# Windowed attention and a maxout FFN on one core: loading q and k chunk by chunk, and splitting attention units by query tile

## The chip, the cores and the metric

The kernel runs on one core of one Trainium2 chip. TensorE (PE) does the matmuls, VectorE (DVE) and ScalarE (ACT) the elementwise work and the copies out of PSUM, GpSimd (POOL) builds the masks and issues most loads, SyncE (SP) issues small copies and the stores. The metric is the device time of one execution in microseconds, lower is better. A profiled execution lists every instruction; its span runs from the first to the last of them.

## The reference

Attention over 4 batches, 8 heads, 768 positions of 64 elements, each query seeing the first 4 positions (sinks) and the last 128; then a feed-forward part with the maximum of three products:

```
scores = (1/8) * q @ k^T
keep   = (key < 4) | (0 <= query - key < 128)
a      = softmax(where(keep, scores, -1e9))
x      = (a @ v) laid out as 3072 tokens x 512
h      = max(x @ w1, x @ w2, x @ w3)          # 512 -> 768
out    = h @ w_out                            # 768 -> 512
```

Inputs and output are float32; the kernel computes in bfloat16 with float32 sums.

## The kernel before, in words

Tokens are cut into 12 chunks of 256 (three a batch). For each chunk there are two attention *units*, one for each group `g` of four heads. A unit's `scores` (L390) writes keys x queries for the four heads into one PSUM tile `st` of four banks, of which there is only one: four heads use four row groups of 32, with even and odd elements of a head dimension as two accumulating passes `e`. Columns 0 to 127 are the previous 128 keys for the first 128 queries, 128 to 383 the first key tile of the chunk for all 256 queries, 384 to 511 the second key tile for the second 128 queries. `exps` (L395, ACT) runs twice, for two heads each, over all columns; `masks` (L403, DVE) likewise multiplies by `mask`, or `mask0` in a batch's first chunk. `pv(tt)` (L412, L421, PE) makes values and row sums for 128 queries; it waits for both masks. `norm` (L431, L434, DVE) divides, `xt` (L444, PE) transposes, `xt_copy` (L451, ACT) stores into `xT`.

Sinks: from a batch's second chunk on, the four sink keys get their own scores (`sink_scores`, L344, exp L350), from `kbd` (L307, DVE), and their values from `vbd`, filled by sixteen small SP copies a batch (`sink_v`, L324).

The FFN works on *blocks* of chunks: `BLOCKS = [[0], [1, 2], [3, 4], [5, 6], [7, 8], [9, 10], [11]]`, so one of 256 tokens, five of 512, one of 256. `hgroup` (L510) makes 18 products a block; the first of each three is copied by ACT (`evac`, L519), the other two are taken into the maximum by DVE (L521). `ygroup` (L529) makes the output of 128 tokens, ACT copies it (L536) and SP stores it. A block's FFN needs the attention of all its chunks; the next block's attention runs beside it. Four PSUM buffers (`h_ring`) serve h, y, values, transposes and sink scores.

q and k must be transposed to put the head dimension on the partitions. DVE does it with 32 x 32 transposes of bfloat16 pairs taken as float32 (L286). Batch 0 is loaded in chunks of 256 tokens (`raw0`); its first chunk comes as float32, by SP for q and ACT for k, four copies for each head group (`qk_first`, L160), with a cast by DVE (L293) for q and ACT (L295) for k. Batches 1 to 3 come as whole loads of 768 tokens for each head group (`batch_loads`, L258), and then three transposes out of the tile, with destination steps of 24 elements where batch 0 has 8. Those loads and v (L172 by key tile in batch 0, L265 by four heads later) are issued by POOL, which casts to bfloat16 on the way.

The order on each engine comes from a planner. Every step is a `Task` with an engine, a cost, what it depends on and a due time `want`; `arrange` takes, over all engines, the task that can start earliest, and among those of one engine that can start about equally early the one with the smallest `want`. Loads are tasks of a model engine `DMA` with 0.30 MB/us (`rate`). Instructions are emitted in the order found, and each engine runs its own in order; at run time semaphores hold them to their true dependencies.

Of the kernel before, what the change touches and what calls it, by code (L numbers as in the profile page):

```python
# [87 lines left out]
def kernel(  # L88
# [35 lines left out]
    mask = const.tile([128, 512], BF16, name="mask")  # L124
# [6 lines left out]
    raw0 = {}  # L131
    for g in range(NQ):
        for nm in "qk":
            raw0["f", nm, g] = const.tile([128, 512], F32, name=f"{nm}_f{g}")
            raw0[nm, g] = const.tile([128, NC, 512], BF16, name=f"{nm}_first{g}")
# [10 lines left out]

    dma_done = {}
    rate = 0.30

    def load(name, mb, want, f, eng="POOL", cost=0.65, deps=()):  # L150
        t = task(eng, cost, f, deps=deps, want=want, name="i" + name)
        dma_done[name] = task("DMA", mb / rate, lambda: None, deps=[t], want=want, lat=2.0, name=name)
# [10 lines left out]
    def qk_chunk(nm, src, g, c):  # L163
        def f():
            s = src[0, 4 * g:4 * g + 4, 256 * c:256 * c + 256].rearrange("i (p j) d -> i p (j d)", j=8)
            nc.gpsimd.dma_start(out=raw0[nm, g][:, c, :], in_=s)
        return f
# [14 lines left out]
    for g in range(NQ):  # L182
        load(f"q0{g}0", 0.26, g - 2000, qk_first("q", q, g), eng="SP", cost=0.4)
        load(f"k0{g}0", 0.26, g - 2000, qk_first("k", k, g), eng="ACT", cost=0.4)
# [8 lines left out]
    for n in range(2):  # L193
        load(f"v0{n}", 0.26, nxt(), v_chunk(n), cost=0.9)
    ws = (moe_w1, moe_w2, moe_w3)
    for wi in range(3):
        load(f"w{wi}0", 0.52, nxt(), w_part(wi, ws[wi], 0, 2))

    def make_masks():
        nc.gpsimd.memset(mask, 1.0)  # L200
        m4 = mask.rearrange("p (t r q) -> p t r q", t=2, r=2)
        nc.gpsimd.affine_select(out=m4[:, :, 1, :], in_=m4[:, :, 1, :], compare_op=ALU.is_ge,
                                fill=0.0, base=0, pattern=[[0, 2], [1, 128]], channel_multiplier=-1)
        nc.gpsimd.affine_select(out=m4[:, :, 0, :], in_=m4[:, :, 0, :], compare_op=ALU.is_gt,
                                fill=0.0, base=0, pattern=[[0, 2], [-1, 128]], channel_multiplier=1)
        nc.gpsimd.tensor_copy(mask0, mask[:, 128:512])
        nc.gpsimd.memset(mask0[0:n_sink, 0:256], 1.0)
# [15 lines left out]
    t_bd = task("POOL", 0.6, make_bd, want=nxt(), name="bd")  # L223

    def chunk_loads(c):
        for g in range(NQ):
            load(f"q0{g}{c}", 0.26, nxt(), qk_chunk("q", q, g, c))
            load(f"k0{g}{c}", 0.26, nxt(), qk_chunk("k", k, g, c))
        for n in (2 * c, 2 * c + 1):
            load(f"v0{n}", 0.26, nxt(), v_chunk(n), cost=0.9)  # L230

    chunk_loads(1)
    for f0 in (2, 4):
        for wi in range(3):
            load(f"w{wi}{f0}", 0.52, nxt(), w_part(wi, ws[wi], f0, 2))
    chunk_loads(2)
    load("wo", 1.57, nxt(), lambda: nc.gpsimd.dma_start(
        out=wo_sb, in_=moe_w_out.rearrange("(a p) f -> p a f", p=128)))

# [5 lines left out]

    t_zero = task("DVE", 3.0, set_zeros, want=-1000, name="zero")


    raws, tr_done, sink_done, qTs = {}, {}, {}, {}
    last_pv = {}  # L250

    def batch_loads(b, after_tr, after_pv):

        for g in range(NQ):
            for nm, src in (("q", q), ("k", k)):
                def f(nm=nm, src=src, g=g):
                    raws[b, nm, g] = io.tile([128, 24, 64], BF16, name=f"{nm}_raw{g}", tag=f"{nm}_raw{g}")
                    nc.gpsimd.dma_start(  # L258
                        out=raws[b, nm, g].rearrange("p j d -> p (j d)"),
                        in_=src[b, 4 * g:4 * g + 4].rearrange("i (p j) d -> (i p) (j d)", j=24))  # L260
                load(f"{nm}{b}{g}", 0.79, nxt(), f, deps=after_tr)
        for hf in range(2):
            def fv(hf=hf):
                vv = vbufs[b % 2][:, 4 * hf:4 * hf + 4, :, :D].rearrange("p h n d -> p (h n) d")
                nc.gpsimd.dma_start(out=vv, in_=v[b, 4 * hf:4 * hf + 4].rearrange(  # L265
                    "h (n p) d -> p (h n) d", p=128))
            load(f"v{b}{hf}", 0.79, nxt(), fv, cost=1.4, deps=after_pv)

    def tile_T(b, nm, g):
        if (b, nm, g) not in qTs:  # L270
            qTs[b, nm, g] = io.tile([128, S, 2], BF16, name=f"{nm}T{g}", tag=f"{nm}T{g}")
        return qTs[b, nm, g]

    def transposes(b, g, part, want):

        for nm in ("q", "k"):
            def f(nm=nm):
                dst = tile_T(b, nm, g).rearrange("p s e -> p (s e)").bitcast(F32)
                if b == 0:
                    src = raw0[nm, g][:, part, :].bitcast(F32).rearrange("p (j c) -> p j c", j=8)  # L280
                    dst = dst[:, 256 * part:256 * part + 256].rearrange("p (m j) -> p j m", j=8)
                else:
                    src = raws[b, nm, g].rearrange("p j d -> p (j d)").bitcast(F32).rearrange(
                        "p (j c) -> p j c", j=24)[:, 8 * part:8 * part + 8, :]
                    dst = dst.rearrange("p (m j) -> p j m", j=24)[:, 8 * part:8 * part + 8, :]
                nc.vector.transpose(dst, src)  # L286
            deps = []
            if b == 0:
                deps.append(dma_done[f"{nm}0{g}{part}"])
                if part == 0:  # L290
                    def cast(nm=nm):
                        if nm == "q":
                            nc.vector.tensor_copy(raw0[nm, g][:, 0, :], raw0["f", nm, g])  # L293
                        else:
                            nc.scalar.copy(raw0[nm, g][:, 0, :], raw0["f", nm, g])  # L295
                    deps = [task("DVE" if nm == "q" else "ACT", 0.5, cast, deps=deps, want=want,
                                 name=f"cast{nm}{g}")]
            else:
                deps.append(dma_done[f"{nm}{b}{g}"])
                if b > 1:  # L300
                    deps += [s_done[b - 2, g, x] for x in range(NC)] + [es_done[b - 2, 1]]
            tr_done[b, nm, g, part] = task("DVE", 0.62, f, deps=deps, want=want,
                                           name=f"tr{nm}{b}{g}{part}")
        if part == 0:
            def sink_k():
                kv = tile_T(b, "k", g)[:, 0:n_sink, :].rearrange("p s e -> p e s")
# [5 lines left out]
            if b > 0:  # L312
                return sink_k
            sink_done[b, "k", g] = task("DVE", 0.2, sink_k, deps=[tr_done[b, "k", g, 0], t_bd, t_zero],
                                        want=want + 3, name=f"kbd{b}{g}")

    def sink_v(b, want):
# [10 lines left out]
        t = task("SP", 1.6, f, deps=deps, want=want, name=f"vbd{b}")  # L328
# [5 lines left out]
    def sink_scores(b, cs, want):  # L334
# [19 lines left out]
        for g in range(NQ):  # L354
            for c in (cs if b == 0 else range(NC)):
                deps.append(tr_done[b, "q", g, c])
        t1 = task("PE", 0.55, mm, deps=deps, want=want, lat=0.2, alloc=[h_ring], name=f"SK{b}{cs}")
# [8 lines left out]
    hs_ring = Ring(2, "hs")  # L366
    h_all, y_all, s_done, chain = {}, {}, {}, {}

    def unit(b, c, g, blk, off, w0, dw):

        lo = 128 if c == 0 else 0
        ncol = 512 - lo
        st = {}

        def scores():
# [3 lines left out]
            qT, kT = tile_T(b, "q", g), tile_T(b, "k", g)  # L379
            q0 = 256 * c  # L380
            parts = []
            if c > 0:
                parts.append((0, 128, q0 - 128, q0))
            parts.append((128, 256, q0, q0))
            parts.append((384, 128, q0 + 128, q0 + 128))
            for col, n, key0, qq in parts:
                for e in range(2):
                    for i in range(4):
                        r = slice(32 * i, 32 * i + 32)
                        nc.tensor.matmul(ps[:, i, col:col + n], lhsT=kT[r, key0:key0 + 128, e],  # L390
# [271 lines left out]
```

## Time and profile before

| | us |
|---|---|
| median of 3 runs (lowest, highest) | 203.46 (203.42, 204.44) |
| the profiled execution | 202.47 |
| its span | 200.7 |
| busy: PE, DVE, ACT, POOL | 172.7, 135.7, 95.1, 36.7 |
| PE busy of the first 16 us | 2.82 |
| mean granted TensorE clock | 0.983 |

A busy PE is not a PE at its peak: a matmul that runs at half clock, or waits inside the pipeline, counts as busy too. So work is priced by stretches in which nothing disturbs it, and holes by what came after them.

### The profile page before, as it was taken

How to read it: one execution, taken by the hardware profiler on the slowest of the kernel's cores; microseconds unless marked ns; L12 is line 12 of the kernel's file. 1: busy time of each engine (PE TensorE's matmuls, PEld its weight loads, DVE VectorE, ACT ScalarE, POOL GpSimd, SP SyncE). 2: the span in 40 equal slices, each digit the busy share in tenths (PEclk: the TensorE clock that was granted, in tenths of full speed). 3: DMA queues.
4: the chain of work that ended last, by engine and by line, in shares of the span. 5: the costliest groups of instructions: out<-in, count | busy, mean ns of one | idle time of the engine just before them, and what ended most of it. 6: DMA issues, size and time to landing. Idle time of an engine off the chain costs nothing.

```text
span 200.7 us, 4228 instructions
## 1 busy us (share of the span) xinstructions
PE 172.7 (86%) x1680; PEld 95.7 (48%) x1680; DVE 135.7 (68%) x290; ACT 95.1 (47%) x146; POOL 36.7 (18%) x56
## 2 busy tenths in 40 slices
PE   0127997588979997999998999989999989999892
PEld 0023676433445544455554455554555544454770
DVE  4358497587999999999917758636677276571450
ACT  0344562634447548434668245665266592223422
POOL 7997648233200000022000000000000000000000
PEclk9999999759999999999999999999999999999999
DMA  7999999999999910409920200140000410002202
GB/s 125 207 160 154 197 172 198 213 180 172 255 173 177 195 63 1 156 4 80 82 106 1 105 4 0 42 170 0 3 0 5 157 52 3 0 0 106 108 0 104
DMA packets 41012, 19.72 MB, mean 98 GB/s; under 512 B 29472, under 2 KB 35872, under 8 KB 40992
## 3 DMA queue, kind: packets, MB, share of 16 engines
q0 software_dynamic: 36256, 12.07, 56.8%
q1 hardware_dynamic: 4352, 6.85, 9.6%
q10 hardware_dynamic: 384, 0.52, 1.0%
q8 instruction: 13, 0.21, 0.4%
q14 instruction: 7, 0.06, 0.1%
HBM read 25.17 MB, written 6.29 MB: 157 GB/s over the span
## 4 chain that ended last, share of the span: by engine, by line
PE 66%; DVE 21%; DMA 5%; issue 3%; ACT 3%; SPq 1%; DVEq 0%; ACTq 0%
PE h L510 39%; PE y L529 13%; PE st L390 6%; DMA q_f<-in_q_dram 5%; DVE kT L286 4%; DVE h_sb L521 4%; DVE x L434 4%; PE o L421 4%; DVE e_sb L403 4%; DVE qT L286 3%; PE xt L444 2%; ACT e_sb L395 2%; PE o L412 2%; DVE rc L431 1%; SPq L160 1%
## 5 line engine op out<-in xcount | busy, mean ns | idle before, releaser
L510 PE MATMUL h<-xT,w_sb 128*128 128x512 bf16 (+1 forms) x504 | 103.7, 353 | 1.8 <-ACT xT L451 1.2
L521 DVE TENSOR_TENSOR h_sb<-h,h_sb 128x512 bf16<-128x512 f32 (+1 forms) x84 | 51.4, 616 | 26.1 <-PE h L510 20.3
L510 PEld LDWEIGHTS <-w_sb 128*128 128x128 bf16 x504 | 46.8, 99 | 38.5 <-issue 2.6
L395 ACT ACTIVATE e_sb<-st 128x1024 bf16<-128x1024 f32 (+1 forms) x48 | 44.4, 953 | 14.4 <-PE st L390 14.4
L519 ACT CAST h_sb<-h 128x512 bf16<-128x512 f32 (+1 forms) x42 | 22.1, 526 | 47.6 <-PE h L510 47.3
L529 PE MATMUL y<-wo_sb,h_sb 128*128 128x512 bf16 x144 | 33.9, 387 | 0.1
L403 DVE TENSOR_TENSOR e_sb<-e_sb,mask 128x1024 bf16<-128x1024 bf16 (+1 forms) x48 | 29.7, 640 | 5.1 <-ACT e_sb L395 4.9
L390 PE MATMUL st<-qT,kT 32*128 32x128 bf16 (+1 forms) x512 | 15.9, 253 | 16.5 <-DVE kT L286 9.3
L536 ACT COPY y_sb<-y 128x512 f32<-128x512 f32 x24 | 14.1, 586 | 21.5 <-PE y L529 17.6
L390 PEld LDWEIGHTS <-kT 32*128 32x128 bf16 x512 | 10.9, 98 | 25.0 <-DVE kT L286 9.9
L434 DVE TENSOR_TENSOR x<-o,rc 128x256 bf16<-128x256 f32 x48 | 20.4, 424 | 1.7
L431 DVE RECIPROCAL rc<-o 128x4 f32<-128x4 f32 x48 | 8.5, 177 | 19.2 <-PE o L421 19.2
L529 PEld LDWEIGHTS <-h_sb 128*128 128x128 bf16 x144 | 13.8, 99 | 15.5 <-issue 1.6
L421 PEld LDWEIGHTS <-e_sb 128*128 128x128 bf16 x352 | 17.4, 102 | 6.5 <-DVE e_sb L403 1.5
L421 PE MATMUL o<-v_sb,e_sb 128*128 128x65 bf16 x352 | 19.4, 201 | 1.1 <-DVE h_sb L521 0.6
L451 ACT COPY xT<-xt 128x512 bf16<-128x512 bf16 x24 | 14.1, 588 | 9.2 <-PE xt L444 9.1
L444 PE MATMUL xt<-ident,x 128*128 128x128 bf16 x96 | 12.3, 230 | 5.1 <-DVE x L434 4.2
L265 POOL DMA_DIRECT2D v_sb<-in_v_dram x6 | 8.5, 1429 | 41.8 <-PE o L421 40.2
L286 DVE STREAM_TRANSPOSE kT<-k_raw 128x256 f32<-128x256 f32 x18 | 13.8, 826 | 0.0
L286 DVE STREAM_TRANSPOSE qT<-q_raw 128x256 f32<-128x256 f32 x18 | 13.7, 820 | 0.0
L444 PEld LDWEIGHTS <-x 128*128 128x128 bf16 x96 | 7.2, 99 | 12.5 <-DVE x L434 8.1
L412 PE MATMUL o<-vbd,e_sink 128*128 128x260 bf16 x32 | 9.2, 287 | 0.0
(35 smaller groups left out, 51.5 us busy)
## 6 DMA issues: line engine op xcount, KB each, us to landing
out_dram<-y_sb SPq DMA_DIRECT2D x24, 256.0 KB
w_sb<-in_moe_w_dram POOLq DMA_DIRECT2D x9, 256.0 KB, 8.4
q_raw<-in_q_dram POOLq DMA_DIRECT2D x6, 384.0 KB, 16.9
k_raw<-in_k_dram POOLq DMA_DIRECT2D x6, 384.0 KB, 16.6
v_sb<-in_v_dram POOLq DMA_DIRECT2D x6, 384.0 KB, 16.0
vbd<-v_sb SPq DMA_DIRECT2D x64, 0.5 KB
v_sb<-in_v_dram POOLq DMA_DIRECT2D x6, 128.0 KB, 7.7
wo_sb<-in_moe_w_out_dram POOLq DMA_DIRECT2D x1, 768.0 KB, 9.8
```

The source lines that it names most:

```text
L286: nc.vector.transpose(dst, src)
L390: nc.tensor.matmul(ps[:, i, col:col + n], lhsT=kT[r, key0:key0 + 128, e], rhs=qT[r, qq:qq + n, e], start=(e == 0), stop=(e == 1))
L395: nc.scalar.activation(st["e"][:, 2 * hh:2 * hh + 2, lo:], st["ps"][:, 2 * hh:2 * hh + 2, lo:], AF.Exp, scale=scale)
L403: nc.vector.tensor_tensor(out=ee, in0=ee, in1=m.unsqueeze(1).to_broadcast([128, 2, ncol]), op=ALU.mult)
L421: nc.tensor.matmul(o[:, i, :], lhsT=st["e"][:, i, col:col + 128], rhs=vbufs[b % 2][:, 4 * g + i, kb, :], start=(c == 0 and n == 0), stop=( ...
L434: nc.vector.tensor_tensor(out=st["x"][:, tt], in0=o[:, :, :D], in1=rc.unsqueeze(2).to_broadcast([128, 4, D]), op=ALU.mult)
L444: nc.tensor.transpose(st["xt"][:, n, 128 * tt:128 * tt + 128], x[:, 128 * n:128 * n + 128], ident)
L451: nc.scalar.copy(xTs[blk][:, 2 * g:2 * g + 2, off:off + 256], st["xt"])
L510: nc.tensor.matmul(ps[:, :ntok], lhsT=w_sb[:, wi, d, fb * 128:fb * 128 + 128], rhs=xTs[blk][:, d, :ntok], start=(d == 0), stop=(d == DSUB ...
L519: nc.scalar.copy(hs, ps[:, :ntok])
L521: nc.vector.tensor_tensor(out=hs, in0=ps[:, :ntok], in1=hs, op=ALU.max)
L529: nc.tensor.matmul(ps, lhsT=box["h"][:, fb, 128 * m:128 * m + 128], rhs=wo_sb[:, fb, :], start=(fb == 0), stop=(fb == FSUB - 1))
```

## The change

It has these parts:

- *Blocks* are given in tiles of 128 tokens and become 256, 256 and then five of 512.
- *Loads of q and k* come chunk by chunk (256 tokens, `qk_chunk`) in all batches, into `raw` tiles with four buffers for each head group; the transposed tiles `qT`, `kT` hold one chunk with four buffers. 36 loads take the place of 12 for batches 1 to 3. The transposes have destination steps of 8 everywhere.
- *The first chunk*: only head group 0 comes as float32 by SP and ACT, with both casts on ACT; head group 1 is the first pair of POOL loads. The mask, now 256 columns instead of 512, is built right behind that pair, ahead of v and the weights.
- *Units by query tile*: `exps(tt)` and `masks(tt)` cover four heads for 128 queries (256 columns a head; 128 for the first tile of a batch), and `pv(tt)` waits for its own tile's mask.
- *The exp table*: a small activation on a cleared tile (`warm`) stands behind the first k loads on ACT.
- *The planner's figures*: rate 0.40, a latency of 4.5 for q and k loads, POOL loads strictly in their order with eight in flight, 11.0 us for the sink copies on SP, stores as tasks of their own with four buffers, and attention spread so that it ends 6 us ahead of its block's end from the third block on.
- A path that would transpose by DMA (`by_dma`) is added, but not used (`FIRST_BY_DMA = 99`).

The core of the diff:

```diff
-            e.dma_start(out=raw0["f", nm, g][32 * i:32 * i + 32, :], in_=s[i])
+            e.dma_start(out=first[nm][32 * i:32 * i + 32, :], in_=s[i])
...
-    rate = 0.30
+    rate = 0.40
...
+        if eng == "POOL":
+            if len(lanes) >= 8:
+                t.deps.append(lanes[-8])
+            t.deps += lanes_i[-1:]
...
+    def qk_loads(ch, g):
+        for nm, src in (("q", q), ("k", k)):
+            deps = [tr_done[nm, ch - NBUF, g]] if ch >= NBUF else []
+            load(f"{nm}{ch}.{g}", 0.26, nxt(), qk_chunk(nm, src, ch, g), deps=deps, lat=4.5)
...
+    qk_loads(0, 1)
     t_mask = task("POOL", 2.1, make_masks, want=nxt(), name="mask")
+    v_loads(0)
+    w_loads(0)
+    t_bd = task("POOL", 0.6, make_bd, want=nxt(), name="bd")
     t_ident = task("POOL", 0.6, make_ident, want=nxt(), name="ident")
...
+    for g in range(NQ):
+        qk_loads(1, g)
+    v_loads(1)
+    w_loads(2)
+    w_loads(4)
+    for g in range(NQ):
+        qk_loads(2, g)
+    v_loads(2)
     load("wo", 1.57, nxt(), lambda: nc.gpsimd.dma_start(
...
+    t_one = task("DVE", 0.1, lambda: nc.vector.memset(warm_sb, 0.0), want=-1001, name="one")
+    task("ACT", 1.5, warm, deps=[t_one], want=-1999, name="warm")
...
+                src = raw(nm, ch, g).bitcast(F32).rearrange("p (j c) -> p j c", j=8)
+                dst = tile_T(nm, ch, g).rearrange("p s e -> p (s e)").bitcast(F32).rearrange(
+                    "p (m j) -> p j m", j=8)
                 nc.vector.transpose(dst, src)
...
+            if ch == 0 and g == 0:
+                def cast(nm=nm):
+                    nc.scalar.copy(raw(nm, 0, 0), first[nm])
...
+        def exps(tt):
+            def f():
+                nc.scalar.activation(st["e"][:, :, cols(tt)], st["ps"][:, :, cols(tt)], AF.Exp, scale=scale)
+            return f
+
+        def masks(tt):
+            def f():
+                ee = st["e"][:, :, cols(tt)]
+                m = mask if c > 0 else mask0[:, 128:384] if tt else mask0[:, 0:128]
+                nc.vector.tensor_tensor(out=ee, in0=ee, in1=m.unsqueeze(1).to_broadcast(list(ee.shape)),
+                                        op=ALU.mult)
...
-            pdeps = list(ms) + chain.get("pv", [])
+            pdeps = [ms[tt]] + chain.get("pv", [])
...
+        for g in range(NQ):
+            if ch >= NC:
+                qk_loads(ch, g)
+                if c == 0 and g == 0:
+                    v_batch(b)
...
-BLOCKS = [[0], [1, 2], [3, 4], [5, 6], [7, 8], [9, 10], [11]]
+BLOCKS = [[0, 1], [2, 3], [4, 5, 6, 7], [8, 9, 10, 11], [12, 13, 14, 15], [16, 17, 18, 19], [20, 21, 22, 23]]
```

The loads of chunk 3 on, and v of the later batches, follow behind `wo` in the order of their chunks: q and k of group 0, in a batch's first chunk its two v loads, then q and k of group 1.

More of the change, by code (lines that the diff above doesn't have):

```diff
@@ L130 @@
     vbufs = [const.tile([128, H, 6, D + 1], BF16, name=f"v_sb{n}") for n in range(2)]
[L131 to L135, printed above, removed]
+    warm_sb = const.tile([128, 2], F32, name="warm")
+    first = {}
+    for nm in "qk":
+        first[nm] = const.tile([128, 512], F32, name=f"{nm}_f")
     tasks = []
@@ L180, in w_part @@
         return f
-    for g in range(NQ):
-        load(f"q0{g}0", 0.26, g - 2000, qk_first("q", q, g), eng="SP", cost=0.4)
-        load(f"k0{g}0", 0.26, g - 2000, qk_first("k", k, g), eng="ACT", cost=0.4)
+    load("q0.0", 0.26, -2000, qk_first("q", q, 0), eng="SP", cost=2.7)
+    load("k0.0", 0.26, -2000, qk_first("k", k, 0), eng="ACT", cost=2.7)
     rank = [-1000.0]
@@ L266, in fv @@
                     "h (n p) d -> p (h n) d", p=128))
[L267 to L276, printed above, removed]
-            def f(nm=nm):
[L278 to L304, printed above, removed]
@@ L459, in unit @@
[L459 to L468 removed]
+            return xTs[blk]
@@ new lines, in unit @@
+        deps = [tr_done["q", ch, g], tr_done["k", ch, g]]
+        n_e = {tt: 4 * (cols(tt).stop - cols(tt).start) for tt in tts}
+        s = task("PE", 0.26 + sum(n_e.values()) / 5000, scores, deps=deps + chain.get("s", []), want=w0,
+                 lat=0.2, alloc=[st_ring, e_ring], name="S" + nm)
+        es = {tt: task("ACT", 0.2 + n_e[tt] / 1280, exps(tt), deps=[s], want=w0 + (0.8 + 0.3 * tt) * dw,
+                       name=f"E{nm}{tt}") for tt in tts}
+        s.users[st_ring] = list(es.values())
@@ L469, in unit @@
+        chain["s"] = [s]
+        s_done[ch, g] = s
+        ms = {tt: task("DVE", 0.1 + n_e[tt] / 1880, masks(tt), deps=[es[tt], t_mask],
+                       want=w0 + (1.3 + 0.4 * tt) * dw, name=f"M{nm}{tt}") for tt in tts}
+        pvs, xs = {}, {}
+        for tt in tts:
+            pdeps = [ms[tt]] + chain.get("pv", [])
             if c > 0:
@@ new lines, with prepare @@
+    starts.append(t0 + len(blocks[-1]) * 5.25)
+    ready = set()
+    def prepare(ch, base, per):
+        if ch in ready:
+            return
+        ready.add(ch)
+        b, c = divmod(ch, NC)
+        for g in range(NQ):
[3 more added lines that the diff above has]
+                    v_batch(b)
+        for g in range(NQ):
+            transposes(ch, g, (base + (g - 1.3) * per, base + (g - 1.2) * per))
+    for n, tiles in enumerate(blocks):
+        length = starts[n + 1] - starts[n]
+        per = (length - (LEAD if n > N0 else 0)) / len(tiles)
+        for ch in sorted(set(t // 2 for t in tiles)):
+            b, c = divmod(ch, NC)
+            tts = [t % 2 for t in tiles if t // 2 == ch]
+            first_tile = 2 * ch + tts[0] - tiles[0]
+            base = starts[n] + first_tile * per
+            step = per * len(tts) / NQ
+            if ch not in ready:
+                prepare(ch, base, step)
```

299 lines of the change are left out of this document (153 added, 146 removed).

## The prediction

> **What bounds the kernel now.** I read the page's busy slices first, then a table of stretches, then the chain that ended last, and only then single rows. The page says where the time is not TensorE's:
>
> ```profile
> span 200.7 us, 4228 instructions
> PE 172.7 (86%) x1680; PEld 95.7 (48%) x1680; DVE 135.7 (68%) x290; ACT 95.1 (47%) x146; POOL 36.7 (18%) x56
> PE   0127997588979997999998999989999989999892
> PEclk9999999759999999999999999999999999999999
> DMA  7999999999999910409920200140000410002202
> GB/s 125 207 160 154 197 172 198 213 180 172 255 173 177 195 63 1 156 4 80 82 106 1 105 4 0 42 170 0 3 0 5 157 52 3 0 0 106 108 0 104
> ```
>
> Each digit covers 5.0 us. PE is full from slice 16 (80 us) on; its holes lie ahead of that, and there the DMA engines are full (slices 1 to 13). The dip of the granted clock at 35 to 45 us follows a hole. By stretches:
>
> ```profile
> 32.00:48.00 16.00, 11.50 (x129) 6.83 (x127) 10.87 (x24) 6.47 (x10) 7.04 (x9) 0.79 1.72 192
> 48.00:80.00 32.00, 29.60 (x320) 15.06 (x319) 31.27 (x65) 18.34 (x28) 3.02 (x5) 1.00 1.16 149
> 80.00:104.00 24.00, 23.93 (x194) 12.03 (x191) 20.30 (x43) 11.48 (x19) 2.85 (x2) 1.00 0.67 90
> 104.00:160.00 56.00, 54.37 (x544) 28.43 (x546) 34.36 (x72) 30.16 (x45) 0.00 (x0) 1.00 0.11 40
> ```
>
> Columns: length, busy PE, PEld, DVE, ACT, POOL, clock, DMA share, GB/s. Three limits follow each other: arrival and order of data up to 48 us, DVE from 48 to 80 (31.3 of 32 us busy), then PE. The chain gives the price of PE work where nothing disturbs it, and the ends of blocks:
>
> ```profile
> 19.74 1.44 PE h L510 x6
> 103.00 1.29 PE y L529 x6
> 124.89 0.57 PE st L390 x24
> 158.51 1.29 PE y L529 x6
> 163.05 12.19 PE h L510 x56
> 180.37 5.20 PE y L529 x24
> 186.75 7.80 PE h L510 x70
> 194.56 2.60 PE y L529 x12
> ```
>
> A block of 512 tokens costs 72 h matmuls at 12.19/56 = 0.218 us (15.7) and 24 y matmuls (5.2): 20.9 us. A block of 256 costs half, 10.4 (7.80 + 2.60). Two steady blocks with four attention units each end 55.5 us apart, 27.75 each, so a unit (one chunk of 256 queries, four heads) costs PE (27.75 - 20.9)/4 = 1.7 us. Twelve 256-token equivalents of FFN (12 x 10.45 = 125) and 24 units (41) make 166 us that no order removes. The rest of the span, some 35 us, is what a reordering can reach: the head, the holes, and a tail of 200.7 - 197.2 = 3.5 us.
>
> **The change, part by part.** *Block cut.* Before: 256, five of 512, 256. After: 256, 256, five of 512. PE's total stays. Work moves: the second block needs chunk 1 only, so its 10.4 us of FFN can run while later loads still travel; the last block is now 512 long with no attention beside it, 20.9 us of dense PE. The same 3.5 us tail remains. A boundary wait like that between 185.57 (180.37 + 5.20) and 186.75, 1.2 us, I keep.
>
> *Head.* What starts the first FFN today:
>
> ```profile
> 5.57 5.71 DMA q_f<-in_q_dram
> 6.21 1.28 ACT L295 ACT_TABLE_LOAD   x1 [6.21 <-DMA k_f<-in_k_dram]
> 12.16 1.50 ACT L395 ACTIVATE e_sb<-st 128x768 bf16<-128x768 f32 x2
> ```
>
> The table load follows the wait for k; loaded behind a small memset it lies under that wait and 1.28 us go. The second q/k set lands at 11.3 and ACT's in-order queue holds the first exps behind its cast until 12.16. After, that set comes bfloat16 through POOL as its first two issues, with no cast behind which anything queues. The q cast moves from DVE to ACT (0.6 more, serial). First scores about 1.2 us earlier; the second set, by an estimate, 7 to 9 instead of 11.3 (the chunk rows below took 8.3 to 10.2 to land in a full queue; this one finds it empty and is issued from about 1 on). On POOL these two issues (0.70 each) and the mask (2.1 by the planner's own cost) now stand ahead of v and the weights, which are issued some 3.5 us later. Sum: first FFN matmuls near 16 instead of 19.7, a gain of 3 to 4 us at that place, zero at the end if the loads below set the next gate. I count zero.
>
> *Loads.* Prices of landing:
>
> ```profile
> 19.45 0.73 POOL L166 DMA_DIRECT2D q_first<-in_q_dram  x1
> q_first<-in_q_dram POOLq DMA_DIRECT2D x1, 128.0 KB, 10.2
> k_first<-in_k_dram POOLq DMA_DIRECT2D x1, 128.0 KB, 8.3
> 22.90 0.67 POOL L166 DMA_DIRECT2D k_first<-in_k_dram  x1 [0.71 <-DMA w_sb<-in_moe_w_dram]
> 26.89 0.82 POOL L237 DMA_DIRECT2D wo_sb<-in_moe_w_out_dram  x1 [0.45 <-DMA w_sb<-in_moe_w_dram]
> wo_sb<-in_moe_w_out_dram POOLq DMA_DIRECT2D x1, 768.0 KB, 9.8
> 31.53 0.54 POOL L258 DMA_DIRECT2D k_raw<-in_k_dram  x1
> k_raw<-in_k_dram POOLq DMA_DIRECT2D x1, 384.0 KB, 12.7
> 33.46 1.44 POOL L265 DMA_DIRECT2D v_sb<-in_v_dram  x1
> v_sb<-in_v_dram POOLq DMA_DIRECT2D x1, 384.0 KB, 16.8
> ```
>
> Issue plus time to landing: wo at 36.7; the four batch-1 q/k loads behind it by 44.2, 1.9 each; the two v loads by 50.3, 3.0 each. Chunk loads (128 KB) landed at 29.65 (q) to 31.2 (the fourth), 0.5 each, and by a third of 1.9 they cost 0.63; I take 0.63. So 36 chunk loads in place of 12 cost DMA nothing: between 24 x (-0.1) and, if the 0.70 us POOL issue became the pace, 36 x 0.07 = 2.5 us, all after the gate. The gate is what block 2 (chunks 2 and 3) needs: chunk 3's q/k for both head groups, with the two v loads between them. wo 36.7 + four chunk loads 2.5 + v 6.1 + 1 for the mask standing ahead of v (between 0 and its 2.1 us) = 46.3.
>
> From landing to the first h of that block, one unit serially: two transposes, scores, exps, the last mask, values, normalisation, transpose, copy:
>
> ```profile
> L521 DVE TENSOR_TENSOR h_sb<-h,h_sb 128x512 bf16<-128x512 f32 x60 | 41.6, 694 | 13.2 <-PE h L510 8.1 <-PE xt L444 2.0 <-ACT xT L451 1.2
> L395 ACT ACTIVATE e_sb<-st 128x1024 bf16<-128x1024 f32 x32 | 32.1, 1024 | 11.6 <-PE st L390 11.5
> L403 DVE TENSOR_TENSOR e_sb<-e_sb,mask 128x1024 bf16<-128x1024 bf16 x32 | 21.2, 685 | 4.1 <-ACT e_sb L395 4.1
> L434 DVE TENSOR_TENSOR x<-o,rc 128x256 bf16<-128x256 f32 x48 | 20.4, 424 | 1.7
> L451 ACT COPY xT<-xt 128x512 bf16<-128x512 bf16 x24 | 14.1, 588 | 9.2 <-PE xt L444 9.1
> L431 DVE RECIPROCAL rc<-o 128x4 f32<-128x4 f32 x48 | 8.5, 177 | 19.2 <-PE o L421 19.2
> L286 DVE STREAM_TRANSPOSE kT<-k_raw 128x256 f32<-128x256 f32 x18 | 13.8, 826 | 0.0
> L286 DVE STREAM_TRANSPOSE kT<-k_first 128x256 f32<-128x256 f32 x6 | 3.7, 623 | 1.2 <-ACT k_first L295 1.2
> L395 ACT ACTIVATE e_sb<-st 128x768 bf16<-128x768 f32 x16 | 12.3, 811 | 2.8 <-PE st L390 2.8
> ```
>
> Exp costs (1024 - 811)/256 = 0.83 ns a column, so 512 columns 0.60. The last tile's values and transposes take half of what a unit's 1.7 leaves beside scores (0.57), 0.56. In order: 1.25 + 0.57 + 1.62 + 0.69 + 0.56 + 0.60 + 0.59, with 0.4 of handoffs (my estimate) 6.3: block 2's FFN starts at 52.6. What PE must have done by then is 2 x 10.4 + 8 x 1.7 = 34 us of work from about 9 on, so it has some 9 us in hand; that cover hides the head's gain and the splitting of exps, and if it goes, H moves one for one.
>
> *Units by query tile.* Exp and mask keep 1024 columns an instruction (chunk 0 of a batch: 512 and 1024 instead of 768 twice, equal sums). Values of the first 128 queries wait for half the exps and masks: about 1.7 us of latency, hidden in PE-full stretches. Nil at the end. What is late next is the single scores buffer, as now.
>
> *Transposes.* 36 of the 48 go from 0.82 to 0.62: 7.2 us of DVE, mainly between 43 and 96 where DVE is full. Per steady block DVE then has 12 h_sb (8.3) + 8 masks (5.5) + 8 normalisations (4.8) + 8 transposes (5.0) + 0.4 = 24.0 of 27.75, 87%. Today 80 to 104 runs at 85% with PE at 99.7%, so I charge nothing.
>
> *Sink rows.* SP's sixteen small copies a batch take as long as before; the planner now books 11.0 instead of 1.6 and sets stores and value matmuls after them. Cost nil while the needed value matmuls come 4 us into block 2 or later; up to 3 us if they come first.
>
> **Sum.** 52.6 + 4 x 27.75 + 20.9 + 3.5 + 1.2 = 189.2 us of span, against 200.7. Outside the span this execution has 202.47 - 200.7 = 1.8: 191.0. The median of the runs (203.46) stands 1.0 above the profiled 202.47; I say 191.5.
>
> **Two rules beside the rows.** The chunk loads landed 0.5 us apart, 8 to 10 us behind their issue, so many were in flight at once. The Trainium skill, "DMA: Bandwidth & Descriptors" (Anatomy of one DMA), gives each such DMA a fixed 2.0 us plus its bytes; taken one after another, 24 more loads would add 48 us, by an estimate from that page; the trace disagrees, since the loads overlap. Its Bandwidth section asks to batch loads to 1 MiB, which speaks against this change and is the second rival's mechanism. The granted clock was 0.79 from 32 to 48, after a hole in PE's work. The skill's "TensorE: Matmul & The Clock Gate" (Part 1) gives idle windows of about 3.4 us as the reason for half rate; the row agrees.
>
> **The rivals.** *Half clock and order while data arrives (0.16).* The planner now assumes 0.40 MB/us where it assumed 0.30; wo, booked for about 32 by its own figures, landed at 36.7. y matmuls of block 0 then stand in PE's order ahead of block 1's h that could run, PE idles, and the next work runs at half rate. For it: the hole before 38 us and its clock. Price: the 9 us in hand and 6 more: block 2 at 59, 197.5 us.
>
> *Chunk loads cost more than their bytes: slower (0.07).* Fourteen chunk loads stand ahead of the gate. If one holds the engines 1.5 us, not 0.63, the gate moves by 14 x 0.87 = 12.2 us, which eats the whole gain (203.7, or 203.2 on the profiled basis); from there on it is slower, about 207 at 1.75. Against it: the landings quoted above.
>
> *DVE as the bound of every block (0.06).* If the split mask, now a strided 256 columns per head, costs 1.1 us and not 0.69, DVE has 27.3 of 27.75 a block and four blocks stretch by 2 each: 199. Against it: the 768-column forms, strided too, lie on the line of the 1024 ones.
>
> *The gate comes earlier (0.09).* If v lands at chunk pace, block 2 starts at 47 as the planner books it: 185.5. For it: the queue moved 125 to 213 GB/s in the first 50 us and 255 once, so the pace can vary.
>
> **How the numbers follow.** Forecast 0.62 (186 to 195: gate between 47.5 and 56), the rivals 0.16, 0.07, 0.06, 0.09. The range 185 to 198.5 leaves out the slower case and the upper ends of the first and third. A measurement of this kernel tells about 0.5% from no change. Faster is all but the slower rival and 0.03 of overlapping stalls that end level: 0.90; same 0.03; slower 0.07.
>
> **What would show it.** In the changed profile: the table load before 5 us; first h near 16; chunk 3's second k landing at 45 to 48; the first 512-column h at 51 to 55; transposes all near 0.62; DVE near 87% and PE near 98% from 55 to 160; y ends about 27.75 apart; masks of 1024 at 0.69. Wrong if PE shows holes behind wo between 30 and 45, or if blocks stand more than 28.5 apart.

## The result and the profile after

The changed kernel takes 197.3 us (median of four runs, 195.0 to 199.0) against 203.4 us before. Two of the four, 195.0 and 196.4, are in its faster state: the ratio, 0.962 [0.952, 0.973], and every difference from the changed kernel given below go by their median, 195.7, and the profiled execution (198.2 us, of which the span is 196.5) is not one of them. The prediction said 191.5 us in a range of 185 to 198.5: the sign and the range hold, the time is 5.8 us off, and most of the reasons below it turn out differently.

The page of the changed kernel, with the same parts as were shown of before (slices of 4.9 us):

```profile
span 196.5 us, 4237 instructions
PE 171.2 (87%) x1659; PEld 95.6 (49%) x1680; DVE 129.1 (66%) x289; ACT 95.5 (49%) x147; POOL 55.7 (28%) x83
PE   0067978399999779999999999999999999999992
PEclk9999999969999969999999999999999999999999
DMA  5999999999999969099992023000041000230014
DMA packets 58964, 19.52 MB, mean 99 GB/s; under 512 B 44352, under 2 KB 55616, under 8 KB 58944
q0 software_dynamic: 54592, 12.40, 71.6%
```

And the last two lines as they stood before the change:

```profile
DMA packets 41012, 19.72 MB, mean 98 GB/s; under 512 B 29472, under 2 KB 35872, under 8 KB 40992
q0 software_dynamic: 36256, 12.07, 56.8%
```

PE now has two holes, at slice 7 (34 to 39 us) and slices 13 and 14 (64 to 74 us), each with a dip of the granted clock behind it. The DMA engines are full to 69 us, as they were before, but then busy again at 74 to 79 and 84 to 103, where before they were full only from 90 to 100. The queue of the software-made loads carries 12.4 MB where it carried 12.1, in 18336 more packets, and the time of its packets is 71.6% of 196.5 = 140.7 us of all 16 engines where it was 56.8% of 200.7 = 114.0. (That is the sum of the packets' times over sixteen. Packets overlap, and the DMA share in the table below goes to 2.22, so it is a measure of cost and not a time for which the engines are taken. It is called the queue's time from here on.) That line is the finding of this case, and it stands in the first page one reads.

The same four stretches as before, same columns:

```profile
32.00:48.00 16.00, 11.76 (x149) 7.40 (x149) 9.73 (x25) 8.60 (x14) 6.66 (x10) 0.89 2.22 172
48.00:80.00 32.00, 29.02 (x317) 16.90 (x321) 25.69 (x64) 16.05 (x25) 14.05 (x19) 0.95 1.41 132
80.00:104.00 24.00, 23.62 (x239) 12.55 (x231) 19.95 (x46) 13.90 (x21) 9.62 (x12) 1.00 1.06 129
104.00:160.00 56.00, 55.52 (x570) 30.02 (x576) 38.92 (x84) 30.98 (x46) 0.00 (x0) 1.00 0.12 41
```

DVE is no longer full between 48 and 80 (25.7 of 32 us, before 31.3), yet PE does not gain there: 3.0 us of it are lost, 2.4 before. What it waits for has changed from DVE's work to data. The timeline's rows for this (start, duration, engine, line, work, in brackets the idle time ahead and what ended it):

```profile
2.68 1.28 ACT L271 ACT_TABLE_LOAD   x1 [2.68 <-issue]
28.49 0.83 POOL L267 DMA_DIRECT2D wo_sb<-in_moe_w_out_dram  x1 [0.97 <-DMA w_sb<-in_moe_w_dram]
34.40 0.70 POOL L188 DMA_DIRECT2D k_raw<-in_k_dram  x1
k_raw<-in_k_dram POOLq DMA_DIRECT2D x1, 128.0 KB, 13.8
38.57 4.44 PE L581 MATMUL y<-wo_sb,h_sb 128*128 128x512 bf16 x11 [3.14 <-DMA wo_sb<-in_moe_w_out_dram]
43.86 2.87 PE L562 MATMUL h<-xT,w_sb 128*128 128x256 bf16 x24
56.69 1.46 PE L562 MATMUL h<-xT,w_sb 128*128 128x256 bf16 x7
60.58 1.03 PE L562 MATMUL h<-xT,w_sb 128*128 128x512 bf16 x4
68.10 0.64 DVE L302 STREAM_TRANSPOSE qT<-q_raw 128x256 f32<-128x256 f32 x1 [4.16 <-DMA q_raw<-in_q_dram]
69.31 0.27 PE L433 MATMUL o<-vbd,e_sink 128*128 128x260 bf16 x1 [1.90 <-DVE h_sb L573]
```

The row without a start is the landing of the load issued at 34.40, chunk 3's second k: 13.8 us later, at 48.2. PE stood 3.14 us before the first y matmul until `wo` landed; block 1's h, which needs no `wo`, came only at 43.9 (its last transposes stood behind that y in PE's order). The first 512-column h is at 57.1, inside the seven matmuls from 56.69. At 64 to 68 us DVE waited 4.16 for a chunk load, with block 2's h evacuations queued behind the transpose, and PE waited for those.

The chain's rows for the ends of the blocks:

```profile
117.54 1.29 PE y L581 x6
144.49 1.29 PE y L581 x6
170.90 1.29 PE y L581 x6
177.21 10.52 PE h L562 x48
188.00 4.93 PE y L581 x22
```

Blocks end at 43.0, 60.7, 92.2, 118.8, 145.8, 172.2 and 192.9. Steady blocks take 26.4 to 27.0 us, and from the end of block 2 to the end of the span it is 104.4 us. All that is in dispute lies ahead of 92 us: block 2 took 31.4 us from y end to y end.

### The profile page after: what moved, and what is told of

Read it like the earlier page. It is cut to its first block, busy times and chain, and to the rows that moved or that the text cites. A ratio compares the mean times of both kernels' runs of the same rounds, so it can differ in the third digit from the quotient of the medians.

```text
span 196.5 us, 4237 instructions
## 1 busy us (share of the span) xinstructions
PE 171.2 (87%) x1659; PEld 95.6 (49%) x1680; DVE 129.1 (66%) x289; ACT 95.5 (49%) x147; POOL 55.7 (28%) x83
## 3 DMA queue, kind: packets, MB, share of 16 engines
q0 software_dynamic: 54592, 12.40, 71.6%
## 4 chain that ended last, share of the span: by engine, by line
PE 47%; DMA 27%; issue 11%; POOL 9%; SPq 3%; DVE 1%; ACT 0%; POOLq 0%; ACTq 0%
PE h L562 29%; DMA q_raw<-in_q_dram 16%; PE y L581 11%; DMA v_sb<-in_v_dram 6%; DMA w_sb<-in_moe_w_dram 5%; SPq L335 3%; PE o L442 3%; PE st L412 2%; POOL w_sb L199 2%; POOL v_sb L290 2%; PE xt L471 2%; POOL q_raw L188 1%; POOL k_raw L188 1%; PE o L433 1%; POOL v_sb L194 1%
## 5 line engine op out<-in xcount | busy, mean ns | idle before, releaser
L562 PE MATMUL h<-xT,w_sb 128*128 128x512 bf16 (+1 forms) x489 | 106.4, 355 | 3.0 <-DMA w_sb<-in_moe_w_dram 1.1
L412 PE MATMUL st<-qT,kT 32*128 32x128 bf16 (+1 forms) x512 | 15.4, 248 | 9.9 <-DVE kT L302 9.8
L302 DVE STREAM_TRANSPOSE qT<-q_raw 128x256 f32<-128x256 f32 x24 | 15.0, 633 | 11.8 <-DMA q_raw<-in_q_dram 11.8
L442 PEld LDWEIGHTS <-e_sb 128*128 128x128 bf16 x352 | 16.9, 99 | 8.9 <-DVE e_sb L424 2.5
L442 PE MATMUL o<-v_sb,e_sb 128*128 128x65 bf16 x352 | 18.9, 197 | 1.6 <-DVE e_sb L424 1.4
L188 POOL DMA_DIRECT2D k_raw<-in_k_dram x23 | 15.6, 678 | 14.0 <-DVE x L461 4.5
L188 POOL DMA_DIRECT2D q_raw<-in_q_dram x23 | 15.9, 691 | 12.9 <-DVE h_sb L573 4.3
L412 PEld LDWEIGHTS <-kT 32*128 32x128 bf16 x512 | 10.2, 96 | 15.0 <-DVE kT L302 9.8
L302 DVE STREAM_TRANSPOSE kT<-k_raw 128x256 f32<-128x256 f32 x24 | 14.7, 627 | 1.1 <-DMA k_raw<-in_k_dram 1.1
L471 PEld LDWEIGHTS <-x 128*128 128x128 bf16 x96 | 7.7, 100 | 9.4 <-DVE x L461 3.6
```

Source lines behind the costliest of these rows:

```text
L188: nc.gpsimd.dma_start(out=raw(nm, ch, g), in_=s)
L412: nc.tensor.matmul(ps[:, i, col:col + n], lhsT=kk[r, k0:k0 + 128, e], rhs=qT[r, q0:q0 + n, e], start=(e == 0), stop=(e == 1))
L442: nc.tensor.matmul(o[:, i, :], lhsT=st["e"][:, i, col:col + 128], rhs=vbufs[b % 2][:, 4 * g + i, kb, :], start=(c == 0 and n == 0), stop=( ...
L471: nc.tensor.transpose(st["xt"][:, n, 128 * tt:128 * tt + 128], x[:, 128 * n:128 * n + 128], ident)
L562: nc.tensor.matmul(ps[:, :ntok], lhsT=w_sb[:, wi, d, fb * 128:fb * 128 + 128], rhs=xTs[blk][:, d, :ntok], start=(d == 0), stop=(d == DSUB ...
```

## The experiments

Two theories at the start. A, the order: the planner books loads at 0.40 MB/us, they come slower, and PE's and DVE's orders put work behind late data. B, the form of the loads: a chunk load (four heads by 256 positions, 128 KB) costs the queue more than its bytes. The page names B's quantity; single packets in the trace say more: a chunk load brings about 400 packets of 4 bytes, a whole-batch load 16 (18752 in all against 3744, where there were 12 whole loads and eight chunk loads). The kernel before, run beside each of these, took 203.1 to 203.6 us.

**e1, the order alone.**

```
-    rate = 0.40
+    rate = 0.30
```

> Theory A (order): the figure 0.40 MB/us books loads 5 to 13 us before they land, so block 0's y stands in PE's order ahead of all of block 1's h, and chunk 6's transposes in DVE's order ahead of block 2's h_sb, and both engines wait. With 0.30 the y come behind 14 of the 18 h groups; A expects no PE wait for wo, block 2's first h at 54 to 55 instead of 57.2, block 2's last y 28 to 30 us later instead of 34.8, and 190 to 192 us. Theory B (load form): the data itself comes late, in whatever order it is used; B expects wo, chunk 3's and chunk 6's loads to land as now and 195 to 198 us.

Measured 195.9 us (193.4 to 197.2), ratio 0.957 [0.949, 0.964]. The wait for `wo` is gone as A said (14 of block 1's 18 h groups now stand ahead of y), but the first 512-column h comes at 58.3 and DVE waits for q loads still:

```profile
L302 DVE STREAM_TRANSPOSE qT<-q_raw 128x256 f32<-128x256 f32 x24 | 14.7, 626 | 8.2 <-DMA q_raw<-in_q_dram 8.1
```

A alone is worth nothing that these runs can tell (195.9 against 195.7; by the ratios 1.1 us, with intervals that overlap), not the 6 us it claimed.

**e2, the form alone.** The chunk loads read 128 rows of 2 KB whose step is one and the same, so that head and position are a single dimension of the source; bytes, tile and place of every load stay. A chunk then holds other positions than it should, so this kernel, and e8 and e12 with the same edit, time the form and don't compute the reference.

```
-            s = src[b, 4*g:4*g+4, 256*c:256*c+256].rearrange("i (p j) d -> i p (j d)", j=8)
-            nc.gpsimd.dma_start(out=raw(nm, ch, g), in_=s)
+            s = src[b, 4*g:4*g+4].rearrange("i (p j) d -> (i p) (j d)", j=24)
+            nc.gpsimd.dma_start(out=raw(nm, ch, g), in_=s[:, 512*c:512*c+512])
```

> Each chunk load reads 128 runs of 2 KB out of the whole batch, so that head and position are one dimension of the source; bytes, number, order and destination of the loads stay, only the positions that a chunk holds differ. Theory B: the 4-byte packets (18752 now, 3744 before) go with the second dimension and so does the extra time; the software queue falls from 71.6% to below 62%, chunk 3's last k lands at 46 instead of 48.2, chunk 6's last q 4 or more us earlier than 68.1, and the time is 190 to 193. Theory A: the order is the same, the loads land within 1 us of now, 196 to 198.

Measured 191.0 us (190.3 to 192.0), ratio 0.935 [0.931, 0.940]: 4.7 us below the changed kernel. Its page:

```profile
span 190.3 us, 4258 instructions
PE   0178988699999999999999999999999999999992
DMA packets 41301, 19.45 MB, mean 102 GB/s; under 512 B 26689, under 2 KB 37953, under 8 KB 41281
q0 software_dynamic: 36928, 12.33, 60.7%
```

The second hole (64 to 74 us) is gone and 17663 small packets with it; the queue's time is 115.6 us, nearly that of before. The wait for `wo` is shorter and still there:

```profile
35.84 5.28 PE L581 MATMUL y<-wo_sb,h_sb 128*128 128x512 bf16 x12 [1.83 <-DMA wo_sb<-in_moe_w_out_dram]
```

So 46 loads of 128 KB cost the queue nearly what the old loads cost (115.6 against 114.0), as the prediction had it, if their rows have one step. Chunk 3's second k lands at 43.8, earlier than either theory said, and still the first 512-column h comes at 55.5.

The edit changes three things at once: the small packets, how many packets a load keeps in flight (last section), and POOL's issue, from 0.68 us a load to 0.56. No run separates them. The issue can't be most of it: that k is issued 0.9 us earlier (33.5 instead of 34.4) and lands 4.4 us earlier.

**e3, fewer loads.** The loads of chunks 6 to 11 are left out.

```
+        ch = ch if ch < 6 else 2 + (ch - 2) % 4
...
+            if ch >= 6:
+                dma_done[f"{nm}{ch}.{g}"] = dma_done[f"{nm}{2 + (ch - 2) % 4}.{g}"]
+                continue
```

> q and k of chunks 6 to 11 are not loaded; their transposes read the tiles of chunks 2 to 5. v stays. This sizes what the late chunk loads cost block 2: both theories expect DVE's 4.2 us wait for chunk 6 and the second half-clock window to vanish and block 2's FFN to take 28 to 30 us instead of 34.8, so 190.5 to 193. A third possibility, that the sink copies on SP hold up block 2, expects it still to take over 33 us, 196 to 198. The wait for wo at 35 to 38.6 stays in all.

Measured 193.9 us (193.3 to 195.2), ratio 0.952 [0.947, 0.957], 1.8 us below the changed kernel. The first 512-column h comes no earlier (59.5), but the block behind it ends at 87.2 instead of 92.2: block 2's hole is the late loads of chunk 6, and between these two profiles that makes 5 us.

**e4, the form in the kernel before.** Its loads of batches 1 to 3 are cut into chunk loads; nothing else changes.

```
-                    nc.gpsimd.dma_start(out=raws[b, nm, g]..., in_=src[b, 4*g:4*g+4].rearrange("i (p j) d -> (i p) (j d)", j=24))
+                    for c in range(NC):
+                        nc.gpsimd.dma_start(out=raws[b, nm, g][:, 8*c:8*c+8, :]...,
+                            in_=src[b, 4*g:4*g+4, 256*c:256*c+256].rearrange("i (p j) d -> i p (j d)", j=8))
```

> The kernel before, with each whole q or k load of batches 1 to 3 replaced by three loads in the chunk form into the same tile (the positions in the tile differ), nothing else. Theory B: each costs 1.1 us and not 0.63; batch 1's last k lands at 48 to 50 instead of 44.2, batch 2's and 3's loads later still; 205 to 209 us. Theory A and the prediction's price (0.63 each): 203 to 204.5 us.

Measured 205.8 us (ten runs, 203.6 to 207.7), ratio 1.0065 [1.0016, 1.0113]: slower by 0.65%, 1.3 us, at the lower end of what B expected.

```profile
q0 software_dynamic: 53536, 12.13, 65.3%
```

That is 133.9 us of the queue against 114.0: the extra 19.9 us, 0.55 for each of the 36 chunk loads, belong to the form and not to the rest of the change (smaller pieces and the second row step together). Here most of it hides behind work.

**e5, whole loads in the changed kernel.** Batches 1 to 3 come in the old loads and are transposed in the old way (a step of 24); a unit then waits for its whole batch.

```
+            elif ch % NC == 0:
...
+                    nc.gpsimd.dma_start(out=raw_whole(nm, ch // NC, g)...,
+                        in_=src[ch // NC, 4*g:4*g+4].rearrange("i (p j) d -> (i p) (j d)", j=24))
...
-        deps = [tr_done["q", ch, g], tr_done["k", ch, g]]
+        deps = [tr_done[x, cc, g] for x in "qk" for cc in ([ch] if b == 0 else range(NC*b, NC*b + NC))]
```

> The changed kernel with the loads and transposes of batches 1 to 3 as before (whole loads of 768 positions, three transposes with steps of 24 each), all else as changed: the chunk-wise part undone alone. Theory B (the chunk form costs DMA time): the 4-byte packets fall below 7000 and the software queue's time from 140.7 to about 122 us; block 2's first h comes later than now (59 to 60, for chunk 3 now waits for three chunks' data), but no load is late after it, so the last y of block 2 ends at 87 to 89 instead of 92.2, and the time is 192 to 194. The prediction's reading, that chunk loads cost their bytes alone and the finer steps are the gain: 198 to 201.

Measured 199.4 us (198.7 to 200.5), ratio 0.980 [0.976, 0.984], as the prediction's reading had it and against B. The queue's time is only 114.7 us, but the first 512-column h comes at 68.4:

```profile
48.90 0.52 PE L445 MATMUL st<-qTb,kTb 32*128 32x256 bf16 x16 [1.32 <-DVE kTb L324]
54.48 0.83 PE L445 MATMUL st<-qTb,kTb 32*128 32x256 bf16 x16 [2.91 <-DVE kTb L324]
```

To load and transpose in chunks is worth 3.7 us even at the price of the form; e9 asks for which chunks.

**e6, the old blocks.**

```
-BLOCKS = [[0, 1], [2, 3], [4, 5, 6, 7], [8, 9, 10, 11], [12, 13, 14, 15], [16, 17, 18, 19], [20, 21, 22, 23]]
+BLOCKS = [[0, 1], [2, 3, 4, 5], [6, 7, 8, 9], [10, 11, 12, 13], [14, 15, 16, 17], [18, 19, 20, 21], [22, 23]]
```

> The changed kernel with the blocks cut as before (256, five of 512, 256). The prediction's theory, that the second small block fills PE while later loads travel: 3 to 6 us slower than the changed kernel, 200 to 203. If the block cut were not what gains: 196 to 198.

Measured 195.5 us (194.7 to 196.4), ratio 0.961 [0.957, 0.964]: not above the changed kernel. The first 512-column h comes at 44.3 and nothing is won or lost by it. The block cut is worth nothing that these runs can tell.

**e7, the split by heads.** Exps, masks and values as before the change.

```
-                nc.scalar.activation(st["e"][:, :, cols(tt)], st["ps"][:, :, cols(tt)], AF.Exp, scale=scale)
+                lo, hh = (128 if c == 0 else 0), slice(2 * tt, 2 * tt + 2)
+                nc.scalar.activation(st["e"][:, hh, lo:], st["ps"][:, hh, lo:], AF.Exp, scale=scale)
...
-            pdeps = [ms[tt]] + chain.get("pv", [])
+            pdeps = list(ms.values()) + chain.get("pv", [])
```

> The changed kernel with exps and masks by two heads over all columns, as before, and values waiting for both masks. The prediction counts the split by query tile as nothing at the end: 196 to 198.5. If the 1.7 us of latency shows wherever PE waits for data: 199 to 201.

Measured 200.6 us (five runs, 200.0 to 202.1), ratio 0.984 [0.981, 0.986]: the split by tiles is worth 4.9 us in this kernel. Not where the expectation looked for it: the first h is 5.6 us later (22.7), but block 2 ends at 91.0, 1.1 us earlier than in the changed kernel's profile. The loss comes behind it: block 3 takes 31.7 us instead of 26.7. DVE's and PE's rows there:

```profile
98.44 0.64 DVE L302 STREAM_TRANSPOSE qT<-q_raw 128x256 f32<-128x256 f32 x1 [2.29 <-DMA q_raw<-in_q_dram]
100.41 0.64 DVE L302 STREAM_TRANSPOSE kT<-k_raw 128x256 f32<-128x256 f32 x1 [1.33 <-DMA k_raw<-in_k_dram]
101.11 0.42 DVE L466 TENSOR_TENSOR x<-o,rc 128x256 bf16<-128x256 f32 x1
101.59 1.04 PE L567 MATMUL h<-xT,w_sb 128*128 128x512 bf16 x4 [3.02 <-DVE x L466]
```

Two transposes wait for loads, a normalisation that PE needs stands behind them, and PE waits 3.02 us. Again late loads; hence e12.

**e12, the split by heads with e2's loads.** Both edits, e2's and e7's.

> The changed kernel with exps, masks and values split by heads as before, and with the chunk loads reading 128 runs of 2 KB out of the whole batch as in e2_merged (a chunk then holds other positions; all sizes and counts of bytes are the same). With the chunk loads as they are, the split by heads cost 3.3 us, and in its profile all of that arises at 98 to 101.6 us, where VectorE stands in transposes that wait for late loads (2.29 and 1.33 us) and PE waits 3.02 for the normalisation behind them. If the split by tiles is worth something by itself (shorter latency of each unit), the loss stays: about 194.3 against 191.0 with merged loads and tiles. If it only mattered through the late loads (the prediction's nil, in a kernel whose loads arrive), the loss goes with them: 190.5 to 192.

Measured 192.0 us (191.6 to 192.4), ratio 0.945 [0.940, 0.950], 1.0 us above e2. Of the 4.9 us, some 4 came through the late loads; what is left, 1.0 (2.0 by the ratios), is at the edge of the two intervals.

**e8, both theories together.** e1's and e2's edits.

> The merged loads (one dimension for head and position) and the planner's figure of 0.30 together. If the order costs by itself (theory A adds to B): no PE wait for wo, 187.5 to 189.5. If the order costs only because data is late: 190 to 192, as with merged loads alone.

Measured 189.1 us (188.5 to 189.7), ratio 0.929 [0.926, 0.932]. With the loads in time, the order is worth another 1.9 us (the runs lie apart, 188.5 to 189.7 against e2's 190.3 to 192.0; the intervals of the ratios just touch); the wait for `wo` is gone, and the clock is full as long as PE works.

```profile
PEclk9999999999999999999999999999999999999999
q0 software_dynamic: 36928, 12.33, 62.8%
```

**e9, a version of use.** Chunk loads for batches 0 and 1, whose first chunks the first blocks wait for, and whole loads with the old transposes for batches 2 and 3, which have time; rate 0.30. It is e5's edit with the first whole batch moved from 1 to 2.

```
-            if ch < NC:
+            if ch < WB * NC:        # WB = 2
```

> The changed kernel with the planner's rate at 0.30, where only batches 0 and 1 come chunk by chunk; q and k of batches 2 and 3 come in the old whole-batch loads (8 loads of 786 KB in place of 24 chunk loads) and are transposed in the old way, eight positions at a time with a step of 24. It computes the reference. The load-form theory: 4-byte packets fall from 18752 to about 9300 (24 x 400 fewer, 8 x 16 more), the software queue's time from 137 (rate 0.30 alone) to about 125 us, chunk 6's transposes no longer wait for a late load, block 2 takes 28 to 30 us instead of 33.7, and the time is 191 to 194 us. The rival (whole loads cost their gate again, as with whole loads from batch 1 on): the units of batch 2 come late, block 3 is held up instead of block 2, 196 us or more. The order theory alone sees no reason for a gain over 195.9.

Measured 191.7 us (191.5 to 192.1), ratio 0.944 [0.940, 0.948], 4.0 us below the changed kernel, and it computes the reference.

```profile
span 190.4 us, 4197 instructions
PE   0047999998598999999999999999999999999992
PEclk9999999999999999999999999999999999999999
DMA packets 47444, 19.48 MB, mean 102 GB/s; under 512 B 34880, under 2 KB 43072, under 8 KB 47424
q0 software_dynamic: 43072, 12.36, 65.3%
L335 DVE STREAM_TRANSPOSE qT<-q_raw 128x256 f32<-128x256 f32 x12 | 7.4, 627 | 4.0 <-DMA q_raw<-in_q_dram 4.0
L326 DVE STREAM_TRANSPOSE qTb<-q_rawb 128x256 f32<-128x256 f32 x12 | 9.3, 806 | 0.0
```

The queue's time is 124.4 us and the wait for q loads half of e1's. Block 2 took 30.2 us (55.7 to 85.9), not quite the 28 to 30 expected.

**e10, the old blocks and rate 0.30.** e1's and e6's edits.

> The changed kernel with the old cut into blocks (256, 512 x 5, 256 tokens) and the planner's rate at 0.30. Either edit alone gave 195.5 and 195.9. If they take away the same wait (PE waiting while the chunk loads trickle in), they don't add: 195 to 196. If the wrong order and the block cut are separate losses, they add: 193 to 194.5.

Measured 195.0 us (194.8 to 196.3), ratio 0.961 [0.956, 0.966]. They don't add: with late loads neither the order nor the cut matters much.

**e11, no early table load.**

```
-    task("ACT", 1.5, warm, deps=[t_one], want=-1999, name="warm")
```

> The changed kernel without the early exponential that loads ACT's table. The table load (1.28 us) then stands right before the first exp. The prediction's reading (a gain of the head is worth nothing, since the end is set by the gate of the first 512-token block): first h about 1.3 us later than 17.04, first 512 h and the end within 0.5 us of the changed kernel, 197.3. The rival (the head is on the path): 198.3 to 198.8.

Measured 196.7 us (193.8 to 198.3), inside the changed kernel's own spread. The first h comes at 18.4 instead of 17.0, 1.35 us later, and the profiled span is 194.6. As far as this spread can tell, this gain at the head is worth nothing at the end, as the prediction counted; whether the loss is within the expected 0.5 us stays open.

Where the gain over the kernel before comes from: undone one at a time, the chunk loads cost 3.7 us (e5) and the split by tiles 4.9 (e7), the block cut, the table load and the planner's rate nothing that can be told. The difference to be explained is 203.4 - 195.7 = 7.7. The first chunk's new path, the mask's place and the planner's other figures were not undone by themselves.

## Why the prediction was right, and where not

- *The sum.* Predicted span 189.2, measured 196.5: 7.3 more. The gate came at 57.1 instead of 52.6 (+ 4.5). From there to block 2's last y it took 35.0 us instead of 27.75 (+ 7.3). The next three blocks took 80.0 instead of 83.25 (- 3.2), the last one and the tail 20.7 + 3.6 instead of 20.9 + 3.5 (- 0.1), and the boundary wait of 1.2 didn't come. The profiled execution lies 2.5 us above 195.7. From block 2's end on it takes 104.4 us, and the profiles of e1, e2, e3, e8 and e9 take 104.0 to 104.5, so by an estimate from these an execution of 195.7 ends block 2 some 2.5 us earlier. The first two terms failed, and not for one reason.
- *Block 2, where the price of a chunk load failed.* "36 chunk loads in place of 12 cost DMA nothing" took 0.63 us by a third of a whole load's 1.9. Without the second row step (e2) the block takes 30.8 us from its first h instead of 35.0, and with the order mended as well (e8) 27.3. By the queue's time the change costs 140.7 - 114.0 = 26.7 us, and e2 takes 25.1 of it back, 0.55 a load over 46 loads. Counted by size in the packet records, a chunk load's own packets took 1.1 us in the changed kernel (0.89 the 1 KB packets, 0.25 the 4-byte ones) and 0.83 in e2, where a third of a whole load had taken 0.67 before. The other 11.2 of the 25.1 us are the 128-byte packets of the v loads, 65.6 us against 54.4; why they take longer beside such loads isn't shown. That e4 gives 0.55 too is luck, for there it is smaller pieces and the step together. So the term is about 1.1 to 1.2 us as these sums count it, between the forecast's 0.63 and the second rival's 1.5. The landings that had priced it, four loads 0.5 us apart, were read with several loads in flight; that this hid the price is argued, not shown.
- *The gate, where the time in hand failed.* Chunk 3's second k landed at 48.2, not 46.3 (+ 1.9), and from there to the first 512-column h it took 8.9 us instead of 6.3 (+ 2.6). The late landing is not all of it: it comes at 43.8 in e2 and at 43.4 in e8, ahead of the forecast, and their gates are still 55.5 and 55.3. What failed is the 9 us that PE was to have in hand. PE was busy 16.2 of the 21.6 us from 17.0 to 38.6, and then, with block 0's y and all of block 1's h still to do, 18.0 of the 18.6 up to the gate. In e8, where most of that h is done before, the k that landed at 43.4 is transposed at 48.4, when its turn comes in DVE's order. No run with this block cut has a gate below 55.3, so what would bring 52.6 stays open. The prediction had named this sign of being wrong, holes of PE "behind wo between 30 and 45": the hole ran from 35.4 to 38.6.
- *The second rival* (chunk loads cost more than their bytes) had the mechanism, with 0.07. The gain was not eaten, since the price is below its 1.5, and since with whole loads (e5) a unit waits still longer.
- *The first rival* (half clock and order, 0.16) came true in its form: PE waits 3.14 us for `wo` with block 1's h behind it, and the clock drops at 39 us. Its price was 6; taking the wait away gains nothing that can be told in e1, and 1.9 in e8. It gave 197.5 and the time is 197.3, which is luck: the loads' form alone is 4.7 of it (e2).
- *Block cut.* Argued as the gain; e6 and e10 give nothing. The early block's FFN didn't fill the time while loads travelled: up to 38.6 PE waited, and most of that block's h came behind it (43.9 on).
- *Units by query tile, "nil at the end".* 4.9 us with the kernel's loads (e7), 1.0 with loads in time (e12). The cover named for it, stretches full of PE, was missing at 98 to 101 us.
- *Head.* First h at 17.0 (near 16), table load at 2.7 (before 5): right, and right to count it zero as far as e11 goes, which undoes 1.35 us of it.
- *Transposes, masks, DVE.* Groups after:

```profile
L573 DVE TENSOR_TENSOR h_sb<-h,h_sb 128x512 bf16<-128x512 f32 (+1 forms) x84 | 51.3, 610 | 35.5 <-PE h L562 32.1
L424 DVE TENSOR_TENSOR e_sb<-e_sb,mask 128x1024 bf16<-128x1024 bf16 (+1 forms) x48 | 29.7, 638 | 2.4 <-ACT e_sb L417 2.4
L302 DVE STREAM_TRANSPOSE qT<-q_raw 128x256 f32<-128x256 f32 x24 | 15.0, 633 | 11.8 <-DMA q_raw<-in_q_dram 11.8
```

Transposes at 0.63 (0.62 said), masks at the old price (0.68 at 1024 columns; 0.64 is a mean over 1024 and 512), DVE never the bound: the third rival is out. DVE was busy 74% from 55 to 160 us where the forecast had 87%: the forecast added up durations, and instructions that stand back to back overlap (a transpose of 0.63 us starts at 48.02, the next at 48.50). The transposes wait 11.8 us for q loads; the group showed 0.0 before (kT) and the idle column of this one row points at the late loads.

- *Steady blocks.* 26.4 to 27.0 instead of 27.75, PE 55.5 of 56 us: right in kind, 1.1 too long each.
- *Gate earlier (0.09).* Not seen in the kernel, nor in any run with this block cut (55.3 in e8 is the earliest).

## What to carry to other kernels

When a load is cut into pieces, price the new form by the queue's total time and packet count, not by a share of the old load's landing: here the own packets of a piece whose rows have one step cost a quarter more than a third of the whole load (0.83 us against 0.67), those of a piece with a second row step 1.7 times as much (1.1), and the loads beside them took longer too. Where engines run in a fixed order, a late load costs more than its own delay, because whatever stands behind the waiting instruction (evacuations behind a transpose, ready h behind y) is late too. An edit can then look worthwhile that is worth little once the load is in time (the split by tiles, 4.9 us and then 1.0), and another shows its worth only then (the order, nothing and then 1.9). While the small form is the dear one, cut into it only what the next gate waits for, and leave the rest whole (e9).

## What the runs showed of the hardware

The packet records of the software queue, counted by size, per 0.5 us at the start, where the two first chunk loads are nearly alone in that queue (in brackets how many 1 KB packets are in flight on the mean):

```
from us       3.0       3.5       4.0       4.5       5.0       5.5       6.0       6.5       7.0
changed: 4 B   84       150       177        90        10         0         0         0       133
        1 KB    7 (2.8)   8 (3.6)  18 (6.6)  30 (7.9)  32 (7.7)  41 (8.9)  36 (8.0)  50 (9.9)  29 (6.4)
e2:      4 B    0         0        15         1        10         6         0         1        15
        1 KB   33 (13.4) 42 (10.7) 55 (11.1) 46 (8.9)  59 (11.5)  5 (1.6)   0         0         0
```

With a second row step, 384 more small packets come with each load, and the last data of the two loads comes behind 7.5 us instead of 5.5. The first load keeps 3 to 4 of its packets in flight, both together about 8; with one step it is 13 for the first. Where only chunk loads stand in the queue, it moved 75 to 120 packets of 1 KB a us (71 to 77 us in the changed kernel) against 158 to 193 (58 to 64 us in e2). The Trainium skill, "DMA: Bandwidth & Descriptors" (Why a DMA increments its semaphore by 16), says that a DMA runs on the largest number of engines, up to 16, that divides the outermost sizes of both its sides: by that rule four for a load with four heads outermost, sixteen for one with 128 rows. The packets in flight agree with it, and so does the semaphore that the first load raises in sixteen steps: in the changed kernel twelve come by 5.1 us and the last four at 7.4 to 7.7, in e2 all sixteen by 5.1. The records name no engine, so that four carried the data is inferred. The section does not say where the small packets come from, and no run here does; it is open too why e2 itself fell to 92 to 96 packets a us from 89 to 92 us.

The Trainium skill, "DMA: Bandwidth & Descriptors" (Bandwidth), asks for loads of 1 MiB and more. In e2, with loads of 128 KB for every chunk, the queue's time is 115.6 us; in e5, with loads of 384 KB for three of four batches, it is 114.7, of which ten chunk loads with a second row step are 5.5 by the 0.55 above. So by an estimate the size is worth about 6 us of the queue's time here, and the second row step 25.
